# Strided and local attention with a layer-normed feed-forward: another order of the prologue and of chunk 0, and one piece of attention moved to chunk 1

## Chip, cores and metric

One core of a Trainium2 chip. The metric is the device time of one execution in microseconds (us); the median of three runs stands for a kernel. Engines: PE (matrix multiplication), DVE (vector), ACT (scalar functions), POOL (GpSimd) and SP, which here only issues DMAs; ACT issues some too. Every engine works its instructions in program order and waits on semaphores.

## The reference

```
scores = q @ k^T / sqrt(64)                      # q, k, v: (8, 8, 576, 64), float32
heads 0..3: keep 0 <= i - j < 32;  heads 4..7: keep j <= i with j % 32 == i % 32
attn = softmax(scores);  out = attn @ v          # heads side by side: x (8, 576, 512)
xn = (x - mean) / sqrt(var + 1e-6) * g_ln
y  = x + relu(xn @ w1) @ w2                      # w1 (512, 2048), w2 (2048, 512), float64
```

w1 and w2 come as float64; the kernel turns them into a high and a low part of float32 on the chip.

## The kernel before

**Pairs.** Attention goes by pairs of heads: 4 pairs in each of 8 batches, numbered 0 to 31, strided and local in turn (pair 0 strided, 1 local, 2 strided, 3 local). **Chunks.** The feed-forward goes by 9 chunks of 512 tokens: chunk c is the first 512 tokens of batch c, the last one what is left over of all batches. In a chunk it goes by 16 blocks f of 128 hidden units. A block is 12 matmuls into one PSUM bank `ph` (8 with the high part of w1, 4 with the low part), relu on ACT (`hh`), the rest on DVE (`hl`), and 12 matmuls into `po`.

**The list.** The prologue (batch 0) and chunk 0 (with batch 1's attention and all of the weights' preparation) follow a string `ORDER` of words `op:k:i:buffer`. Each word emits one step, and since every engine keeps program order, the list is each engine's order. The words:

- `T` turn the rows of q (i=0) or k (i=1) of pair k on PE, `c` copy them out of PSUM; `r` load raw q and k of a later pair, `tp` transpose them on DVE; `v` load v, `vs` copy v shifted by a block on POOL;
- `S` scores on PE, `mask`, `max` on DVE, `sub` (minus the maximum) on POOL, `exp` on ACT, `PP` transpose the probabilities on PE, `pt` copy them, `V` probabilities times v on PE, `den`, `xo` divide on DVE, `X` transpose the output on PE, `xh`, `xl` its high and low part, `st` store it;
- `W` load block k of both weights, and for weight i: `sc` scale the upper word on ACT, `low`/`lowA` shift the lower word on DVE or ACT, `mg` and `sg` put number and sign together on DVE, `hi` the high part on ACT, `lo` the low part on POOL; for w1 also `byg` (times g) and `add` (block sum) on POOL, `cm` column mean on PE, `cen` subtract it on DVE;
- `F` the 8 high matmuls of block k (`Fb` the last two of block 0, which need pair 3), `H` the 4 low ones, `hh`, `hl`, `G` the 12 matmuls of the block's second half; `xr`, `xs` the residual and its scale.

PSUM gives the prologue three rooms of two banks (buffers 0, 1, 2); a step that takes a room waits until the last reader of that room is done. There is one bank for `ph`.

**Before the list** stand the loads of batch 0: rows of q on SP and of k on ACT for pairs 1 to 3, pair 0's halves on both, then `gcol` and all of v on SP.

**Pieces.** From chunk 1 on a generator `pieces()` works batch 2 and later ones: in every block f one visit, after the block's first half (`ffn1`, `hh`, `hl`) and ahead of the second half of the block before. A piece i spans four visits: in the first S of pair i+1 and V of pair i on PE, mask to exp for pair i+1, the store of pair i and the load of v for pair i+2; in the second `x_raw` (pair i back from DRAM), the sums and the turn of pair i+1's probabilities through DRAM (`p_turned`), the transposition of q and k of pair i+3 and the load for pair i+4; in the third the load of the turned probabilities (`p_load`) and `x_blocks`; the fourth is empty. The first piece is i = 8; pair 8's scores and the turn of its probabilities (on PE, `PP:8`) stand in the list of chunk 0.

Of the kernel before, what the change touches and what calls it, by code (L numbers as in the profile page):

```python
# [26 lines left out]
hi:0:0 lowA:2:0 mg:1:0 hi:0:1 lo:0:0 F:0 exp:4 den:3 sg:1:0 lowA:3:0 lo:0:1 xo:3 sc:1:1 low:1:1
byg:1 X:3::1 mg:1:1 v:4 sg:1:1 add:1 PP:4::2 xh:3 sc:2:0 xl:3 cm:1::0 mg:2:0 Fb:0 pt:4 lowA:3:1
W:4 cen:1 H:0 lowA:2:1 sg:2:0 hi:1:0 tp:5 byg:2 V:4::0 hh:0 sc:2:1 add:2 hl:0 S:5::1 hi:1:1 st:1
mg:2:1 lo:1:0 cm:2::2 sg:2:1 F:1 W:5 mask:5 sc:3:0 lo:1:1 hi:2:1 cen:2 H:1 mg:3:0 hi:2:0 G:0  # L30
sg:3:0 hh:1 den:4 W:6 sc:3:1 hl:1 lowA:4:1 mg:3:1 lo:2:0 byg:3 lowA:4:0 F:2 sg:3:1 add:3 xo:4
sc:4:0 hi:3:1 W:7 mg:4:0 H:2 lo:2:1 lowA:5:0 sg:4:0 cm:3::0 G:1 cen:3 byg:4 sc:4:1 hi:3:0 mg:4:1
add:4 hh:2 sg:4:1 st:4 hl:2 sc:5:0 X:4::0 lo:3:0 F:3 mg:5:0 xh:4 r:6 lo:3:1 lowA:5:1 xl:4 H:3
sg:5:0 cm:4::0 hh:3 G:2 cen:4 byg:5 sc:5:1 hl:3 lowA:6:1 v:5 add:5 mg:5:1 hi:4:0 sg:5:1 lowA:6:0
lo:4:0 F:4 max:5 sc:6:0 lowA:7:0 mg:6:0 sub:5 lowA:7:1 cm:5::0 sg:6:0 H:4 cen:5 W:8 sc:6:1 byg:6
G:3 hh:4 mg:6:1 add:6 hi:4:1 hl:4 hi:5:0 sg:6:1 lo:5:0 cm:6::0 sc:7:0 F:5 cen:6 W:9 exp:5 lo:4:1
mg:7:0 hi:5:1 sg:7:0 H:5 tp:6 byg:7 sc:7:1 PP:5::0 lowA:8:0 G:4 add:7 st:0 hh:5 hi:6:0 hl:5 lo:5:1
pt:5 r:7 mg:7:1 hi:6:1 S:6::0 lo:6:0 sg:7:1 lowA:9:0 lowA:8:1 F:6 mask:6 sc:8:0 max:6 cm:7::0
mg:8:0 sg:8:0 sub:6 H:6 st:3 G:5 hh:6 cen:7 byg:8 st:2 hl:6 hi:7:0 lo:6:1 tp:7 sc:8:1 hi:7:1
V:5::0 add:8 lowA:9:1 r:8 F:7 mg:8:1 sg:8:1 lo:7:0 den:5 sc:9:0 xo:5 H:7 mg:9:0 sg:9:0 cm:8::0  # L40
hh:7 G:6 exp:6 byg:9 hl:7 W:10 sc:9:1 cen:8 add:9 mg:9:1 hi:8:0 PP:6::0 hi:8:1 sg:9:1 lo:8:0 F:8
tp:8 pt:6 W:11 lo:7:1 hi:9:1 cm:9::0 H:8 lo:8:1 sc:10:0 cen:9 lowA:10:0 G:7 lowA:10:1 mg:10:0 W:12
hi:9:0 sg:10:0 hh:8 byg:10 sc:10:1 hl:8 S:8::0 lowA:11:0 lo:9:0 mg:10:1 F:9 lowA:11:1 sg:10:1 v:6
add:10 mask:8 sc:11:0 H:9 mg:11:0 lo:9:1 lowA:12:1 sg:11:0 cm:10::0 G:8 hh:9 cen:10 byg:11 W:13
sc:11:1 hi:10:0 mg:11:1 hi:10:1 lo:10:0 hl:9 lowA:12:0 S:7::0 sg:11:1 add:11 sc:12:0 F:10 mask:7
W:14 lo:10:1 mg:12:0 cm:11::0 sg:12:0 H:10 max:7 sc:12:1 byg:12 G:9 hh:10 cen:11 st:5 add:12
mg:12:1 hi:11:0 hl:10 lowA:13:1 W:15 lo:11:0 sg:12:1 hi:11:1 cm:12::0 F:11 max:8 sc:13:0 lowA:13:0
cen:12 H:11 mg:13:0 hi:12:0 v:7 sg:13:0 lo:12:0 X:5::0 hh:11 G:10 xh:5 lo:11:1 sc:13:1 xl:5
lowA:14:1 hl:11 sub:7 hi:12:1 mg:13:1 V:6::0 lowA:14:0 r:9 byg:13 F:12 sg:13:1 den:6 add:13 xo:6
sc:14:0 H:12 lo:12:1 lowA:15:0 mg:14:0 exp:7 cm:13::0 sg:14:0 G:11 hi:13:1 cen:13 byg:14 xr:0  # L50
hh:12 sc:14:1 hl:12 lo:13:1 hi:13:0 mg:14:1 X:6::0 lo:13:0 sg:14:1 F:13 xh:6 add:14 xr:1 sc:15:0
xl:6 H:13 sub:8 mg:15:0 cm:14::0 hh:13 G:12 cen:14 xr:2 sg:15:0 hi:14:0 hl:13 byg:15 xs:0 PP:7::0
lo:14:0 F:14 pt:7 tp:9 st:6 lowA:15:1 add:15 sc:15:1 H:14 r:10 cm:15::0 hh:14 G:13 cen:15 exp:8
hl:14 hi:14:1 mg:15:1 hi:15:0 sg:15:1 lo:15:0 V:7::0 hi:15:1 xr:3 F:15 lo:15:1 den:7 xo:7 lo:14:1
xs:2 X:7::0 v:8 H:15 G:14 hh:15 xh:7 hl:15 xl:7 v:9 tp:10 PP:8::0 pt:8 xs:3 st:7 r:11 xs:1
# [972 lines left out]
```

## Time and profile before

| | us |
|---|---|
| median of 3 runs | 911.18 (909.15 to 911.70) |
| span of the profiled execution | 907.3 |
| median less span | 3.9 |
| PE busy | 884.9 |
| DVE, ACT, POOL busy | 435.4, 199.7, 147.9 |

The page comes from one profiled execution. PE's busy time counts overlapping matmuls once. The timeline lists instructions of one engine in order of time, and in square brackets how long the engine was idle before one and what ended that; "issue" means that it waited for nothing that the profile shows.

### The profile page before, as it was taken

The page shows a single profiled execution, that of the slowest core. Times are in us where ns is not written, and L with a number is a line of the kernel's source. Part 1 is how long each engine was busy: PE and PEld are TensorE (multiplying, and loading weights), DVE is VectorE, ACT ScalarE, POOL GpSimd, SP SyncE. Part 2 cuts the span into 40 slices and gives each one's busy share as a digit, 9 for nine tenths or more (in the row PEclk, how much of TensorE's full clock was granted, in tenths as well). Part 3 has the DMA queues.
Part 4 walks back from the last instruction along what each step waited for, and adds up shares of the span by engine and source line. Part 5 has one row for each costly group of instructions (what it writes and reads, how often), then busy time and mean ns, then how long its engine had stood idle before and what let it go on. Part 6 is the DMA issues. An engine that isn't in the chain of part 4 may idle for free.

```text
span 907.3 us, 18531 instructions
## 1 busy us (share of the span) xinstructions
PE 884.9 (98%) x7606; PEld 728.8 (80%) x7606; DVE 435.4 (48%) x864; ACT 199.7 (22%) x326; POOL 147.9 (16%) x186
## 2 busy tenths in 40 slices
PE   7699999999999999999999999999999999999997
PEld 6578787888888888888888888888888888888885
DVE  2888877544654455445644464445533321132113
ACT  3477663111111111111111111111111111111110
POOL 5477774000100011000100010001000000000000
PEclk8999999999999999999999999999999999999999
DMA  8887886675867575766666665757443230002001
GB/s 166 226 257 179 247 196 114 147 111 119 134 142 109 102 137 120 124 91 141 109 134 93 135 104 141 100 127 124 116 85 91 49 128 0 1 1 93 0 1 47
DMA packets 339621, 102.98 MB, mean 114 GB/s; under 512 B 276944, under 2 KB 331344, under 8 KB 339536
## 3 DMA queue, kind: packets, MB, share of 16 engines
q1 hardware_dynamic: 249920, 85.53, 42.9%
q10 hardware_dynamic: 89616, 16.26, 11.5%
q8 instruction: 60, 0.98, 0.5%
q14 instruction: 25, 0.20, 0.1%
...
## 4 chain that ended last, share of the span: by engine, by line
PE 93%; DMA 2%; DVE 1%; issue 1%; SPq 1%; POOL 1%; ACT 0%; DVEq 0%; POOLq 0%; ACTq 0%
PE po L775 42%; PE ph L748 28%; PE ph L755 14%; PE m L515 2%; PE m L445 2%; DMA s<-in_moe_w_ch_dram 1%; PE t L371 1%; PE s L445 1%; DMA rows<-in_q_dram 1%; PE av L515 1%; SPq L351 1%; PE cm L281 1%; PE px L636 0%; PE pp L501 0%; POOL r L270 0%
## 5 line engine op out<-in xcount | busy, mean ns | idle before, releaser
L775 PE MATMUL po<-w,hh 128*128 128x512 f32 x1152 | 359.2, 393 | 0.0
L765 DVE SCALAR_TENSOR_TENSOR hl<-ph,hh 128x512 fp32r<-128x512 f32 x144 | 99.3, 690 | 367.0 <-ACT hh L760 367.0
L775 PEld LDWEIGHTS po<-w,hh 128*128 128x128 f32 x1152 | 213.4, 188 | 44.8
L748 PE MATMUL ph<-xh,w 128*128 128x512 f32 x576 | 226.0, 392 | 1.4 <-ACT w L294 1.2
L775 PE MATMUL po<-w,hl 128*128 128x512 f32 x576 | 224.5, 390 | 0.0
L748 PE MATMUL ph<-xl,w 128*128 128x512 f32 x576 | 224.5, 390 | 0.0
L760 ACT ACTIVATE hh<-ph 128x512 fp32r<-128x512 f32 x144 | 86.1, 598 | 483.7 <-PE ph L755 469.0
L755 PE MATMUL ph<-xh,w 128*128 128x512 f32 x576 | 155.3, 392 | 0.0
L748 PEld LDWEIGHTS ph<-xh,w 128*128 128x128 f32 x576 | 108.3, 188 | 24.1 <-ACT w L294 1.4
L775 PEld LDWEIGHTS po<-w,hl 128*128 128x128 f32 x576 | 108.1, 188 | 23.1
L755 PEld LDWEIGHTS ph<-xh,w 128*128 128x128 f32 x576 | 108.2, 189 | 22.5 <-POOL w L298 0.2
L748 PEld LDWEIGHTS ph<-xl,w 128*128 128x128 f32 x576 | 108.3, 188 | 22.0
L491 POOL TENSOR_TENSOR sm<-sm,mx 128x648 f32<-128x648 f32 (+1 forms) x32 | 40.6, 1269 | 440.4 <-DVE mx L486 440.4
L723 POOL TENSOR_TENSOR rs<-rs,mhalf 128x1 f32<-128x1 f32 x36 | 19.7, 548 | 286.5 <-DVE rs L722 286.5
L497 ACT ACTIVATE sm<-sm 128x648 f32<-128x648 f32 (+1 forms) x32 | 23.8, 742 | 104.3 <-POOL sm L491 104.3
L298 POOL TENSOR_TENSOR w<-r,w 128x512 fp32r<-128x512 f32 x32 | 41.1, 1297 | 7.3 <-ACT w L294 6.9
L687 DVE TENSOR_TENSOR xl<-xo,xh 128x512 fp32r<-128x512 f32 x24 | 16.6, 692 | 38.8 <-ACT xh L686 38.8
L686 ACT ACTIVATE xh<-xo 128x512 fp32r<-128x512 f32 x24 | 15.2, 632 | 62.0 <-DMA pd<-sm 18.2
L486 DVE TENSOR_REDUCE mx<-sm 128x12 f32<-128x648 f32 (+1 forms) x32 | 26.3, 822 | 2.1
L565 DVE TENSOR_TENSOR xo<-m,den 64x64 f32<-64x64 f32 (+3 forms) x120 | 27.1, 289 | 0.0
L781 DVE SCALAR_TENSOR_TENSOR x<-po,rs,x 128x512 f32<-128x512 f32 x36 | 24.5, 737 | 2.0 <-PE po L775 1.8
L718 DVE BATCH_NORM_STATS2 st<-x 128x6 f32<-128x512 f32 x36 | 24.3, 674 | 0.0
...
## 6 DMA issues: line engine op xcount, KB each, us to landing
...
```

Source lines behind the costliest of these rows:

```text
L298: nc.gpsimd.tensor_tensor(out=t[:, 1], in0=self.w[i], in1=t[:, 0].bitcast(F32), op=ALU.subtract)
L445: nc.tensor.matmul(o, lhsT, rhs, start=True, stop=True, tile_position=(64 * h, pos))
L486: nc.vector.reduce_max(mx[:, :, 0:nt], sm, axis=AX.X)
L491: nc.gpsimd.tensor_tensor(out=sm, in0=sm, in1=mx[:, :, 0:nt].unsqueeze(3).broadcast_to([P, 2, nt, sm.shape[3]]), op=ALU.subtract)
L515: nc.tensor.matmul(at(h, t)[m * j:m * (j + 1)], self.p_cols(rows, t, j), self.v[rows, n, 0:w], start=True, stop=True, tile_position=(64 * ...
L565: nc.vector.tensor_tensor(out=xo[r, t0:t1, h0:h1].rearrange("p t h d -> p h t d"), in0=av, in1=den[r, h0:h1, t0:t1].unsqueeze(3).broadcast_to(
L748: nc.tensor.matmul(ph, w1h[:, cc], x[:, cc, :], start=(new and n == 0 and i == 0), stop=False)
L755: nc.tensor.matmul(ph, w1l[:, cc], xt[c][0][:, cc, :], start=False, stop=(cc == NCC - 1))
L760: nc.scalar.activation(out=hh, in_=ph, func=AF.Relu)
L765: nc.vector.scalar_tensor_tensor(out=hl, in0=ph, scalar=0.0, in1=hh.bitcast(F32), op0=ALU.max, op1=ALU.subtract)
L775: nc.tensor.matmul(po[i], hx[:, cs], w, start=(f == 0 and n == 0), stop=(f == NFC - 1 and n == 2))
L781: nc.vector.scalar_tensor_tensor(out=x, in0=po[i], scalar=rs, in1=x, op0=ALU.mult, op1=ALU.add)
```

## The change

All of `ORDER` is a new list. With it:

- the loads of batch 0 are words of the list now: `R` loads rows (pair 0's in halves on SP and ACT as before, k first; all others on SP), `g` loads `gcol`, `v` loads v; block 0 of the weights is loaded right behind the rows of pair 1;
- some steps go to DVE by a `D` behind the word: `cD` (two copies of turned rows), `addD` (block sum of block 0), `loD` (two low parts);
- pair 8's `S` to `pt` leave the list; piece 7, which has no pair of its own, does its scores in chunk 1's first visit, and its probabilities go through DRAM like those of later pairs. The pieces up to 11 have three visits, so chunk 1 holds five; the transposition and the load in the second visit are for pairs i+2 and i+3.

```diff
-T:0:0:0 T:0:1:1 c:0:0: c:0:1: T:1:0:2 S:0::0 c:1:0: T:1:1:2 mask:0 max:0 T:2:1:0 c:1:1: sub:0
+R:0:1 R:0:0 T:0:1:1 cD:0:1: R:1:1 T:0:0:0 c:0:0: T:1:1:2 R:1:0 S:0::0 mask:0 c:1:1: W:0 low:0:0
+max:0 T:1:0:1 R:2:1 sc:0:0 c:1:0: S:1::0 R:2:0 v:0 lowA:0:1 mg:0:0 sub:0 exp:0 sg:0:0 sc:0:1 T:2:1:2
...
     def m_piece(p, nxt):
-        ps = bank(f"m{p.id}")
+        ps = bank(f"m{(p or nxt).id}")
         parts = nxt.s_blocks(ps) if nxt else None
-        if p.k == 2 * NHP:
-            p.v_sums()
-        av = p.v_blocks(ps)
+        av = p.v_blocks(ps) if p else None
...
-    for p in first:
-        if p.k in BY_DVE:
-            p.load_qk(early.tile([P, 2 * S], F32, name=f"raw{p.id}"))
-        elif p.k == 0:
-            for i in range(2):
-                p.load_rows(i, nc.sync, slice(0, 1))
-                p.load_rows(i, nc.scalar, slice(1, 2))
-        else:
-            p.load_rows(0, nc.sync)
-            p.load_rows(1, nc.scalar)
-    nc.sync.dma_start(gcol, g_ln.rearrange("(c p) -> p c", p=P))
-    for p in first:
-        p.load_v(once=True)
...
     def one(op, k, i, buf):
         p = pairs[k]
-        if op == "T":
+        eng, copy = nc.gpsimd, nc.scalar.copy
+        if op.endswith("D"):
+            op, eng, copy = op[0:-1], nc.vector, nc.vector.tensor_copy
+        if op == "R":
+            if k == 0:
+                p.load_rows(i, nc.sync, slice(0, 1))
+                p.load_rows(i, nc.scalar, slice(1, 2))
+            else:
+                p.load_rows(i, nc.sync)
...
     def pieces():
-        for i in range(2 * NHP, NP):
+        for i in range(2 * NHP - 1, NP):
+            now = pairs[i] if i >= 2 * NHP else None
...
-            if i + 3 < NP:
-                pairs[i + 3].t_piece()
-            if i + 4 < NP:
-                pairs[i + 4].load_qk()
+            if i + 2 < NP:
+                pairs[i + 2].t_piece()
+            if i + 3 < NP:
+                pairs[i + 3].load_qk()
             yield
...
-            yield
+            if i >= 3 * NHP:
+                yield
```

Three places show what stands in a row now. **SP's queue at the start**; `rows_2`, `rows_0`, `rows_3`, `rows_1` are the rows of pairs 0, 1, 2, 3 (the names count heads), `s_` the weights, `raw_2` q and k of pair 4. Before:

```order
L361 DMA rows_2_235<-in_q_dram 96x3x128
L361 DMA rows_2_235<-in_k_dram 96x3x128
L361 DMA rows_0_240<-in_q_dram 96x6x128
L361 DMA rows_3_243<-in_q_dram 96x6x128
L361 DMA rows_1_246<-in_q_dram 96x6x128
L813 DMA gcol<-in_moe_g_ln_dram 128x4x1
```

After:

```order
L360 DMA rows_2_235<-in_k_dram 96x3x128
L360 DMA rows_2_235<-in_q_dram 96x3x128
L360 DMA rows_0_254<-in_k_dram 96x6x128
L360 DMA rows_0_254<-in_q_dram 96x6x128
L222 DMA s_0_311<-in_moe_w_ch_dram 128x4x256
L225 DMA s_0_312<-in_moe_w_ch_dram 128x1024
L360 DMA rows_3_331<-in_k_dram 96x6x128
L360 DMA rows_3_331<-in_q_dram 96x6x128
```

Pair 1's k rows moved from ACT to SP, block 0 of the weights came up to stand behind pair 1, and v stands behind pair 2's rows.

**ACT's queue around the first relu** (`hh_0`); `w_1` is block 1's high part (the first of the two is w1's), `s_` and `p_` the weights' words in preparation. Before:

```order
L251 ACTIVATE s_3_765<-s_3_765 128x512
L251 ACTIVATE s_2_709<-s_2_709 128x512
L294 ACTIVATE w_1_905<-r_1_848 128x512
L760 ACTIVATE hh_0_935<-ph_0_838 128x512
L244 ACTIVATE p_2_937<-s_2_709 128x512
```

After:

```order
L292 ACTIVATE w_2_914<-r_2_910 128x512
L242 ACTIVATE p_3_916<-s_3_781 128x512
L249 ACTIVATE s_3_781<-s_3_781 128x512
L755 ACTIVATE hh_0_933<-ph_0_897 128x512
L292 ACTIVATE w_1_935<-r_1_720 128x512
```

The first steps on block 3 (`p_3`, `s_3`) stand right ahead of `hh_0` and of block 1's high part now.

**DVE's queue from `hl_1` to `hl_2`**, which frees the bank for the next block. Before:

```order
L765 SCALAR_TENSOR_TENSOR hl_1_1048<-ph_1_994,hh_1_1038 128x512
L258 SCALAR_TENSOR_TENSOR p_3_1046<-p_3_1046,s_3_765 128x512
L264 SCALAR_TENSOR_TENSOR r_3_1064<-s_3_765,p_3_1046 128x512
L565 TENSOR_TENSOR xo<-av_910,den_213 128x2x6x64
L258 SCALAR_TENSOR_TENSOR p_4_1069<-p_4_1069,s_4_893 128x512
L264 SCALAR_TENSOR_TENSOR r_4_1084<-s_4_893,p_4_1069 128x512
L284 TENSOR_TENSOR r_3_1036<-r_3_1036,cm_1086 128x512
L258 SCALAR_TENSOR_TENSOR p_4_1102<-p_4_1102,s_4_894 128x512
L264 SCALAR_TENSOR_TENSOR r_4_1111<-s_4_894,p_4_1102 128x512
L765 SCALAR_TENSOR_TENSOR hl_2_1115<-ph_2_1055,hh_2_1109 128x512
```

After:

```order
L760 SCALAR_TENSOR_TENSOR hl_1_1057<-ph_1_1012,hh_1_1052 128x512
L256 SCALAR_TENSOR_TENSOR p_4_1054<-p_4_1054,s_4_870 128x512
L262 SCALAR_TENSOR_TENSOR r_4_1076<-s_4_870,p_4_1054 128x512
L483 TENSOR_REDUCE mx_0_1082<-sm_208 128x2x5
L256 SCALAR_TENSOR_TENSOR p_4_1109<-p_4_1109,s_4_871 128x512
L262 SCALAR_TENSOR_TENSOR r_4_1122<-s_4_871,p_4_1109 128x512
L663 TENSOR_TENSOR xl_1119<-px_1084,xh_1118 128x30x16
L663 TENSOR_TENSOR xl_1119<-px_1084,xh_1118 128x2x16
L256 SCALAR_TENSOR_TENSOR p_5_1131<-p_5_1131,s_5_886 128x512
L262 SCALAR_TENSOR_TENSOR r_5_1155<-s_5_886,p_5_1131 128x512
L760 SCALAR_TENSOR_TENSOR hl_2_1160<-ph_2_1091,hh_2_1139 128x512
```

Preparation runs about one block further ahead of the relus, and pair 4's low part `xl` stands between them earlier.

## Rows read from the trace of the kernel before

**Rows 1.** The page: busy time of each engine, its share of the span, instructions.

```profile
PE 884.9 (98%) x7606; PEld 728.8 (80%) x7606; DVE 435.4 (48%) x864; ACT 199.7 (22%) x326; POOL 147.9 (16%) x186
```

**Rows 2.** PE's timeline, 0 to 60 us: start, duration, instructions, [idle before <-releaser].

```profile
8.28 1.21 PE L371 MATMUL t<-ident,rows 96*64 96x96 f32 x24 [1.68 <-DMA rows<-in_q_dram]
...
16.28 0.88 PE L445 MATMUL s<-kt_l,qt_l 64*32 64x64 f32 x38 [3.09 <-issue]
...
28.65 0.76 PE L515 MATMUL av<-v_l,pt 64*32 64x65 f32 x52 [1.27 <-issue]
29.21 0.99 PE L445 MATMUL s<-kt_l,qt_l 64*32 64x64 f32 x75
33.03 0.31 PE L445 MATMUL s<-kt_l,qt_l 64*32 64x64 f32 x5 [2.83 <-issue]
...
37.89 0.77 PE L501 MATMUL pp<-ident,sm 128*128 128x128 f32 x5 [1.78 <-ACT sm L497]
...
44.27 0.50 PE L748 MATMUL ph<-xh,w 128*128 128x512 f32 x1 [1.19 <-ACT w L294]
...
54.70 0.47 PE L748 MATMUL ph<-xh,w 128*128 128x512 f32 x1
```

**Rows 3.** Busy us by stage: PE, PEld, DVE, ACT, POOL (instructions), PE's clock, DMA, GB/s.

```profile
5.30:54.70 49.40, 34.47 (x929) 28.87 (x925) 30.20 (x52) 26.08 (x40) 24.04 (x33) 0.86 0.87 208
54.70:92.20 37.50, 37.50 (x295) 30.68 (x294) 32.56 (x51) 26.44 (x46) 30.34 (x33) 1.00 0.79 211
92.20:155.20 63.00, 62.72 (x536) 50.53 (x527) 48.31 (x83) 35.50 (x61) 42.32 (x44) 1.00 0.79 191
```

**Rows 4.** Groups by line and shape, 5 to 60 us: busy us, mean ns.

```profile
L258 DVE SCALAR_TENSOR_TENSOR p<-p,s 128x512 uint32<-128x512 uint32 x8 | 5.5, 687 | 0.2
...
L667 DVE TENSOR_TENSOR xl<-px,xh 128x512 fp32r<-128x512 f32 x2 | 1.4, 680 | 0.0
...
L251 ACT ACTIVATE s<-s 128x512 uint32<-128x512 uint8 x6 | 3.8, 669 | 0.0
...
L383 ACT COPY qt_s<-t 128x576 f32<-128x576 f32 x2 | 2.5, 1240 | 5.0 <-PE t L371 5.0
...
L407 POOL COPY v_l<-v_l 32x1088 f32<-32x1088 f32 x4 | 4.4, 1109 | 0.2
L491 POOL TENSOR_TENSOR sm<-sm,mx 128x648 f32<-128x648 f32 x3 | 3.8, 1273 | 8.6 <-DVE mx L486 8.6
```

**Rows 5.** Timelines of ACT and SP, 0 to 60 us: the issue of loads (start, duration).

```profile
1.21 2.95 ACTq L361 DMA_DIRECT2D rows<-in_k_dram  x4
4.20 1.28 ACT L383 ACT_TABLE_LOAD   x1 [4.20 <-DMA rows<-in_q_dram]
```

**Rows 6.** Moved GB/s in 40 slices of 0 to 42 us.

```profile
GB/s 0 42 250 272 213 231 227 208 231 214 230 161 120 86 50 219 152 130 73 151 207 241 378 350 181 128 28 137 128 140 345 392 327 418 388 383 388 229 42 128
```

**Rows 7.** DMA queues from 30.0 to 33.1 us: PE's instruction queue (packets, MB).

```profile
q8 instruction: 1, 0.02, 2.7%
```

**Rows 8.** Timelines of PE and ACT in chunk 1: S, V, and the loads of `pt`.

```profile
178.99 0.91 PE L445 MATMUL m<-kt_s,qt_s 64*64 64x54 f32 x44
179.83 0.97 PE L515 MATMUL m<-v_l,pt 64*32 64x64 f32 x72
...
202.72 0.97 PE L445 MATMUL m<-kt_l,qt_l 64*32 64x64 f32 x72
...
192.09 2.42 ACTq L628 DMA_DIRECT2D pt<-pd  x4
...
218.06 0.38 ACTq L623 DMA_DIRECT2D pt<-pd  x1
```

More of the change, by code (lines that the diff above doesn't have):

```diff
@@ L27 @@
[L27 to L55, printed above, removed]
-"""
-BY_DVE = ()
@@ L59 @@
-ONCE = False
+R:0:1 R:0:0 T:0:1:1 cD:0:1: R:1:1 T:0:0:0 c:0:0: T:1:1:2 R:1:0 S:0::0 mask:0 c:1:1: W:0 low:0:0
+max:0 T:1:0:1 R:2:1 sc:0:0 c:1:0: S:1::0 R:2:0 v:0 lowA:0:1 mg:0:0 sub:0 exp:0 sg:0:0 sc:0:1 T:2:1:2
+mask:1 mg:0:1 sg:0:1 R:3:0 max:1 PP:0::0 c:2:1: T:2:0:1 cD:2:0: pt:0 sub:1 V:0::0 T:3:0:2 g:0 den:0
+byg:0 hi:0:1 c:3:0: xo:0 R:3:1 addD:0 S:2::1 X:0::2 cm:0::0 mask:2 T:3:1:1 exp:1 xh:0 max:2 cen:0
+PP:1::0 lo:0:1 c:3:1: sub:2 S:3::1 r:4 hi:0:0 pt:1 exp:2 xl:0 v:1 tp:4 PP:2::0 lo:0:0 pt:2 W:1
@@ new lines @@
+S:4::2 mask:3 lowA:1:0 vs:1 sc:1:0 max:3 mask:4 v:3 mg:1:0 V:1::0 v:2 W:2 den:1 sg:1:0 xo:1 sub:3
+lowA:1:1 exp:3 sc:1:1 mg:1:1 r:5 PP:3::2 max:4 X:1::0 sg:1:1 V:2::1 pt:3 W:3 vs:3 xh:1 den:2 hi:1:1
+xo:2 lowA:2:0 sc:2:0 v:4 V:3::2 X:2::1 xl:1 den:3 byg:1 mg:2:0 sub:4 exp:4 xh:2 lo:1:1 xo:3 PP:4::0
+W:4 lowA:2:1 W:6 sg:2:0 X:3::2 W:5 sc:2:1 xl:2 add:1 mg:2:1 F:0 xh:3 xl:3 pt:4 cm:1::2 sg:2:1 Fb:0
+hi:2:1 sc:3:0 H:0 W:7 tp:5 cen:1 lowA:3:0 byg:2 add:2 hh:0 hi:1:0 mg:3:0 S:5::0 cm:2::2 V:4::1 hl:0
@@ new lines @@
+sg:3:0 lo:2:1 lo:1:0 F:1 cen:2 lowA:3:1 sc:3:1 lowA:4:0 den:4 st:3 mask:5 H:1 xo:4 byg:3 hi:2:0
+add:3 lowA:4:1 cm:3::0 W:8 mg:3:1 sg:3:1 hh:1 sc:4:0 cen:3 hl:1 G:0 hi:3:1 mg:4:0 sg:4:0 lo:2:0
+hi:3:0 lowA:6:0 max:5 X:4::0 F:2 r:6 sc:4:1 st:0 st:1 lo:3:1 mg:4:1 byg:4 xh:4 sg:4:1 lowA:5:0 xl:4
+sub:5 add:4 lo:3:0 sc:5:0 lowA:6:1 mg:5:0 H:2 hh:2 G:1 cm:4::0 sg:5:0 byg:5 hi:4:1 hl:2 sc:6:0 F:3
+mg:6:0 st:2 low:7:1 lowA:5:1 sg:6:0 add:5 v:5 H:3 cen:4 exp:5 cm:5::0 G:2 lowA:7:0 sc:7:0 hi:4:0 W:9
+hh:3 mg:7:0 sg:7:0 sc:5:1 cen:5 low:8:0 hl:3 byg:6 mg:5:1 lowA:8:1 sg:5:1 lo:4:1 add:6 byg:7 lo:4:0
@@ new lines @@
+cm:6::0 F:4 hi:5:0 H:4 sc:7:1 cen:6 lo:5:0 hi:5:1 mg:7:1 PP:5::0 sg:7:1 hi:6:0 tp:6 G:3 sc:8:0
+mg:8:0 hh:4 sg:8:0 pt:5 hl:4 sc:6:1 add:7 st:4 hi:7:1 W:10 lo:6:0 S:6::0 F:5 mg:6:1 mask:6 lo:5:1
+byg:8 sg:6:1 max:6 cm:7::0 cen:7 lo:7:1 H:5 sc:8:1 W:11 G:4 sub:6 mg:8:1 hi:6:1 hi:7:0 sg:8:1
+low:9:0 hh:5 sc:9:0 add:8 V:5::0 hl:5 mg:9:0 hi:8:1 sg:9:0 den:5 lowA:9:1 exp:6 lo:7:0 lo:8:1 sc:9:1
+lowA:10:0 xo:5 byg:9 mg:9:1 r:7 sg:9:1 F:6 cm:8::0 cen:8 sc:10:0 H:6 hh:6 W:12 add:9 hi:9:1 mg:10:0
+sg:10:0 lowA:10:1 lo:6:1 G:5 sc:10:1 lowA:11:0 hi:8:0 hl:6 PP:6::0 mg:10:1 lo:9:1 pt:6 F:7 byg:10
@@ new lines @@
+lo:8:0 H:7 sg:10:1 sc:11:0 low:11:1 cm:9::0 G:6 hi:10:1 mg:11:0 sg:11:0 lo:10:1 cen:9 add:10 hh:7
+sc:11:1 mg:11:1 byg:11 hi:9:0 lowA:12:0 lo:9:0 W:13 hl:7 cm:10::0 sg:11:1 tp:7 add:11 F:8 cen:10
+st:5 H:8 sc:12:0 S:7::0 hi:11:1 mg:12:0 low:12:1 sg:12:0 G:7 mask:7 hi:10:0 sc:12:1 mg:12:1 hh:8
+lowA:13:0 hl:8 sg:12:1 W:14 lowA:13:1 sc:13:0 lo:11:1 cm:11::0 cen:11 byg:12 F:9 mg:13:0 H:9 lo:10:0
+sg:13:0 W:15 add:12 hi:12:1 max:7 lowA:14:0 sc:13:1 cm:12::0 hi:11:0 mg:13:1 lowA:14:1 byg:13 cen:12
+sg:13:1 G:8 hh:9 hl:9 X:5::0 sc:14:0 sub:7 hi:12:0 hi:13:1 lo:11:0 F:10 H:10 add:13 loD:12:1 mg:14:0
@@ L368, in t_rows @@
             for a in range(NA):
-                for c in range(2):
+                for c in range(CC):
                     for h in range(2):
@@ L906, in one @@
         elif op == "lo":
-            split(k).rest(i)
+            split(k).rest(i, eng)
         elif op == "F":
@@ L939, in pieces @@
             yield
-            pairs[i].x_raw(nc.scalar)
+            if now:
+                now.x_raw(nc.scalar)
             if nxt:
@@ L950, in pieces @@
                 nxt.p_load()
-            pairs[i].x_blocks()
+            if now:
+                now.x_blocks()
             yield
-            yield
+            if i >= 3 * NHP:
+                yield
     gen = pieces()
```

74 lines of the change are left out of this document (39 added, 35 removed).

## Prediction, made without the result

> **What bounds the kernel now.** I read the page first, then the matmul engine's (PE's) timeline, then the busy time by stage, then the queues. The page gives a span of 907.3 us, and PE is busy 98% of it [rows 1]. PE's timeline shows that all of its waits over 0.3 us lie ahead of 54.70, where the second feed-forward block of chunk 0 (F:1) starts without a wait [rows 2]; from 54.7 to 92.2, the start of F:7, PE is busy 37.50 of 37.50 us, and from there to the first visit of chunk 1 at 155.2 62.72 of 63.00 [rows 3]. From 5.3 to 54.7 it is busy only 34.47 of 49.40 us [rows 3]. So the end moves by four things alone: when F:1 starts, new waits after it, PE work that is added or dropped, and new waits in chunk 1. The time outside the span is 911.18 - 907.3 = 3.9 us against the median of the three runs, and I add it unchanged.
>
> **Term 1: the start of F:1.** PE has the same work ahead of F:1 in both lists, so what changes is waiting. I follow the longest chain through the new list, with the durations of [rows 4].
>
> The first load: before, S:0 stands behind T:1:0, which waits for its q rows until 8.28 and takes 1.21 [rows 2], so S:0 can't start before 9.4. After, T:1:1 stands there, whose load is the first behind pair 0's. ACT issues two loads instead of five (five took until 4.16), so its table load of 1.28 ends near 3.0 and not 5.5 [rows 5]. T:0:1 is copied on DVE (a price that no row shows: between 0.68, DVE reading as many PSUM columns densely, and 1.24, ACT's price for this strided copy; I take 0.95, and nobody waits for it). The q copy on ACT ends near 7.9, S:0 starts at 8.0, mask and max end at 11.3 with the shift of W:0 between them, the subtraction on POOL (1.27) at 12.8, the exponential at 13.6.
>
> S:1 needs T:1:0 and ends near 14.5, with a wait of 3 us in it as before; before it ended at 17.2 [rows 2]. From there the matrices go round three PSUM rooms. With 0.15 us for each hand-over, PP:0 starts at 15.8, V:0 at 18.0, S:3 ends at 27.0 (before 33.3), and PP:3 starts at 31.6 (37.89) [rows 2]. The gain comes mostly from T:2 and T:3, each cut into halves between other work, and from the shifted copies of v on POOL (2 x 1.11 each [rows 4]), which now stand behind the subtractions that gate the chain.
>
> Then DVE carries the chain, almost without a gap: den, xo, the second max, the halves of x, until xl:2 at 42.4 and xl:3 at 43.7. F:0 starts at 41.2 (44.27 [rows 2]), H:0 ends at 45.1, cen:1 on DVE ends at 46.4, hi:1:0 on ACT at 47.0, V:4 on PE at 47.8, and F:1 starts at 48.0 instead of 54.70: 6.7 us.
>
> Does the data come in time? ACT's queue is the place that decides: sc:3:0 and lowA:3:0 now stand ahead of hh:0 and hi:1:0, so F:1 waits for W:3 to land. Up to W:3 SP moves 2.36 MB of rows, 1.18 of v, 1.18 of raw q and k (pair 5's load of 0.59 moved ahead of W:3) and 4.19 of weights: 8.9 MB. Before, the core moved 208 GB/s on average from 5.3 to 54.7 [rows 3], and 220 to 270 for the first rows, 350 to 420 for weights [rows 6]. At 208 that is 42.8 us after the first issue at about 0.7, and with some 1.5 for the first and last latency W:3 lands at about 45. Four ACT steps of about 0.67 [rows 4] follow: F:1 at 48. The two chains arrive together, with no slack between them. A walk leaves out all small gaps, so I take **1.0** off: **-5.7** us.
>
> Three of PE's waits before are put down to "issue": 3.09, 1.27 and 2.83 us [rows 2]. One 16 KB packet of PE's instruction queue lies in the stretch of the last one [rows 7], and between the second and the third stand 52 + 75 matmuls, each with its weight load: 254 instructions. The new list has the same small matmuls, so I keep such waits in it, of 1.3 to 3 us each, in S:1, S:3, V:1 and V:3; of the last three some 3 us in all lie on the chain, the rest beside work of DVE and POOL. The Trainium skill ("Runtime: NRT & Kernel Launch", Instruction fetch mechanics) says that the sequencer fetches the next 16 KiB block of 256 instructions while it executes the current one and that crossing a boundary is mostly hidden; the trace disagrees for runs of such short matmuls, with 7.2 us of waits, and by that rule the sum would be some 3 us lower.
>
> **Term 2: from F:1 to F:7.** There is one PSUM bank for ph, so F:k+1 waits until DVE has read ph for hl:k. Before, DVE is busy 32.56 of 37.50 us in this stretch with 51 instructions [rows 3]. The new list puts more preparation ahead of F:7: four magnitudes, three signs and one centring more (8 x 0.69 = 5.5 [rows 4]), one more den and xo (1.2), three shifts on DVE (1.5), one pair of local transposes less (-1.5). That makes 39.3 us of DVE for 37.5 + 0.9 = 38.4 us of PE (one more V block). So DVE becomes the bound here by about 0.9, and its own idle time (4.9 us before; most of it vanishes when it is the bound) adds something. I take **+1.5**; bounds 0 and +4. After F:7 DVE has 5 us less to do than before, and was busy only 48.31 of 63.00 us [rows 3], so nothing more is lost there.
>
> ACT and POOL carry about the same as before; what moves to DVE (one block sum, two rests) relieves POOL at places where PE isn't waiting.
>
> **Term 3: PE work.** The six transposes of PP:8 go (0.6 to 0.7), the copy pt:8 on ACT too; S:8 only moves from chunk 0 into the first visit of chunk 1. In exchange pair 8's probabilities take the way through DRAM that all later pairs take. **-0.65**.
>
> **Term 4: chunk 1 in visits of three.** Before, S of one piece starts at 178.99 and of the next at 202.72 [rows 8], four visits apart; without the 1.8 us of S and V that is 5.48 a visit, so with three the next V comes 18.3 us after this one. A strided pair's pt load is issued on ACT from 192.09 to 194.5, a local one's at 218.06 [rows 8]; with three visits V would want them at 179.83 + 18.3 = 198.1 and 203.6 + 18.3 = 221.9, so 3.6 and 3.5 us after the last issue. The landing itself isn't in the trace. A local load is 320 KB on a shared queue: 1.5 us at 220 GB/s, 3 at half of it, plus latency. So it is near the edge: 0 to 1 us for each of four pieces. I take **+0.8**, bounds 0 and +4. Pair 8's own load stands behind chunk 0's four stores on SP, but v's loads are ahead of them and there is no store of pair 7's output any more. From chunk 2 on all is one visit earlier, which gives slack.
>
> **Sum:** -5.7 + 1.5 - 0.65 + 0.8 = -4.05: a span of 903.2, and **907.1 us** as measured.
>
> **Rivals.**
> (a) DVE as bound keeps its old rhythm. If it is busy only 87% (32.56 of 37.50) also when it has 39.3 us to do, F:1 to F:7 takes 45.2 us instead of 38.4: +6.8 in place of +1.5, less what DVE gains by running ahead when PE is late (some 2.5). 910 us. Against it: DVE idles now mostly because it waits for PE.
> (b) Chunk 1's three visits are too short: 3.6 us do not cover the pt load, each of four pieces loses 1 us: +4 in place of 0.8: 910.3.
> (c) The one queue is late, and this one ends slower. All rows now go through SP but for pair 0's, and 1.05 MB of weights stand ahead of T:2's. If the 8.9 MB come at 170 GB/s instead of 208, W:3 lands at 54.5, F:1 starts at 57.2, term 1 is +2.5, term 2 vanishes, and with terms 3 and 4 the time is 913.8. It decides against the change below about 180 GB/s. For it: v's loads ran at 50 to 160 GB/s for most of 11.5 to 20 us [rows 6]. Against it: their packets are small and SP was busy issuing them, while weights on the same single queue reached 350 to 420.
> (d) PE's instruction blocks are there in time in the new order: no waits in S:3, V:1, V:3, 3 us less: 904. The mechanism needs PE to be slower than the fetch, and only three of the seven blocks fetched up to 60 us show a wait before. This is what the rule of the Trainium skill cited in term 1 would give.
> (e) The change doesn't do what it says. Read in the code, it does: piece 7 with no pair of its own, then 3 visits each up to piece 11, 15 of chunk 1's 16 visits. No chance of its own.
>
> **How the numbers follow.** The forecast 0.52 (own range 904 to 909), (a) 0.18, (b) 0.10, (c) 0.13, (d) 0.07. A measurement tells about 0.3% from no change, 2.7 us: faster is below 908.45, slower above 913.9. Of the forecast 0.45 lies below that bound; (d) lies below it whole, (a) and (b) by 0.03; that is 0.55 faster. Of (c) most lies above 913.9, with its worse cases: 0.11 slower. The rest, 0.34, is the same. For eight in ten the range runs from the forecast with (d)'s gain and no loss in terms 2 and 4, 902, to the near side of (c), 912.5.
>
> **What would show it.** Right: F:1 at 47 to 50, hh:0 not waiting for W:3 longer than 1 us, DVE busy over 90% between F:1 and F:7, PE waits for hl of 1 to 2 us in total there, V in chunk 1 with waits of under 1 us each. Wrong: F:1 after 52 (then see whether ACT's sc:3:0 waits for DMA, or PE for "issue"), PE idle between F:1 and F:7 of over 4 us, or a wait of PE for pt in chunk 1 of over 2 us.

## Result and the profile after

The changed kernel takes 922.15 us (median of 4 runs, 921.26 to 924.36), the kernel before 910.16 in the same comparison: ratio 1.0149 [1.0120, 1.0177], so 13.5 us slower by the ratio (the two medians alone differ by 12.0). The forecast was 907.1, in a range of 902.0 to 912.5. The profiled span went from 907.3 to 921.0 us. Page of after, busy time of the engines, beside [rows 1]:

```profile
PE 888.6 (96%) x7600; PEld 730.6 (79%) x7600; DVE 440.9 (48%) x874; ACT 196.5 (21%) x321; POOL 145.2 (16%) x182
```

PE's busy time grew by 3.7 us with less work to do, so 10 of the 13.7 us of span are idle time and the rest is matmuls that take longer. After: PE's waits by what ended them (us in total, times, longest), the first five of the list:

```profile
PE po L770 <- DVE x L776: 7.0, 5, 1.4
PE s L442 <- issue: 4.7, 1, 4.7
PE pp L498 <- DVE r L282: 3.8, 2, 3.5
PE av L511 <- issue: 3.0, 2, 1.6
PE m L511 <- DMA pt<-pd: 2.9, 4, 0.9
```

The first, third and fifth are new. Where they stand in the span is seen best from one marker, the start of the relu `hh` on ACT (us). At chunk 2, block 1 both kernels have done the same pairs, apart from the six transposes of `PP:8`:

| `hh` of | before | after | after less before |
|---|---|---|---|
| chunk 0, block 1 | 57.73 | 56.24 | -1.5 |
| chunk 0, block 10 | 115.91 | 113.76 | -2.2 |
| chunk 0, block 12 | 128.64 | 132.16 | +3.5 |
| chunk 2, block 1 | 257.96 | 263.33 | +5.4 |
| chunk 3, block 1 | 353.09 | 360.24 | +7.2 |
| chunk 7, block 1 | 730.68 | 744.28 | +13.6 |

**The prologue.** After, PE's timeline in S:1, and from V:4 to F:1 (start, duration, [idle before <-releaser]):

```profile
11.31 0.87 PE L442 MATMUL s<-kt_l,qt_l 64*32 64x64 f32 x66 [0.74 <-ACT qt_l L379]
16.91 0.46 PE L442 MATMUL s<-kt_l,qt_l 64*32 64x64 f32 x14 [4.72 <-issue]
...
51.83 0.92 PE L511 MATMUL av<-v_s,pt 54*64 54x65 f32 x46 [0.64 <-DMA v_s<-in_v_dram]
52.68 0.50 PE L743 MATMUL ph<-xh,w 128*128 128x512 f32 x1
```

F:1 starts at 52.68, not at 48.0 (54.70 before [rows 2]). S:1 comes to its stop earlier than before (12.2 against 13.2) and leaves it later (16.91 against 16.28 [rows 2]). In either kernel the stop is behind PE's 222nd matmul, and the DMA records show what comes just ahead of its end: one 16 KB packet of PE's own instruction queue, from 13.69 to 15.11 us here and from 13.48 to 14.69 before. After, that queue from 13.6 to 15.2 us (packets, MB, share of 16 engines):

```profile
q8 instruction: 1, 0.02, 5.5%
```

From F:1 to F:7 (after, busy us of PE, PEld, DVE, ACT, POOL, PE's clock, DMA, GB/s):

```profile
52.68:91.18 38.50, 38.50 (x307) 31.60 (x302) 36.65 (x59) 29.11 (x51) 34.36 (x37) 1.00 1.00 276
```

DVE is at 95% there, and PE doesn't wait at all.

**The end of chunk 0.** After, PE and then DVE around `PP:7`:

```profile
129.09 1.33 PE L498 MATMUL pp<-ident,sm 128*128 128x128 f32 x5 [3.45 <-DVE r L282]
130.07 2.05 PE L750 MATMUL ph<-xh,w 128*128 128x512 f32 x4
```

```profile
127.34 0.69 DVE L713 BATCH_NORM_STATS2 st<-x 128x6 f32<-128x512 f32 x1 [4.09 <-DMA x<-xds]
...
128.36 0.68 DVE L282 TENSOR_TENSOR r<-r,cm 128x512 f32<-128x512 f32 x1
```

DVE stands idle for 4.09 us until the residual of `xs:1` has landed; behind it in program order is `cen:14` (L282), which empties the PSUM room that `PP:7` needs. The residual's loads were issued at 120.0 to 122.2. Behind the wait PE is slow as well: the granted clock is 0.83 from 126 to 136, a mean of its two levels, 1.2 and 2.4 GHz; it is at the lower one from 128.7 to 132.2.

**The start of every later chunk.** After, PE and DVE at the start of chunk 2:

```profile
262.17 1.07 PE L750 MATMUL ph<-xh,w 128*128 128x512 f32 x4
264.63 0.70 PE L770 MATMUL po<-w,hh 128*128 128x512 f32 x2 [1.40 <-DVE x L776]
```

```profile
260.31 0.79 DVE L606 STREAM_TRANSPOSE sm<-sm 128x640 f32<-128x640 f32 x1
261.02 1.22 DVE L417 STREAM_TRANSPOSE qt_s<-raw 128x576 f32<-128x576 f32 x1
262.08 1.24 DVE L417 STREAM_TRANSPOSE kt_s<-raw 128x576 f32<-128x576 f32 x1
263.16 2.64 DVE L776 SCALAR_TENSOR_TENSOR x<-po,rs,x 128x512 f32<-128x512 f32 x4
```

Before, PE (S and V of the visit in block 0, then chunk 2's first `po`) and DVE at the same place:

```profile
250.25 0.97 PE L445 MATMUL m<-kt_l,qt_l 64*32 64x64 f32 x72
251.15 1.04 PE L515 MATMUL m<-v_s,pt 54*64 54x64 f32 x44
...
257.70 0.62 PE L775 MATMUL po<-w,hh 128*128 128x512 f32 x2
```

```profile
255.19 2.71 DVE L781 SCALAR_TENSOR_TENSOR x<-po,rs,x 128x512 f32<-128x512 f32 x4
```

`finish` (L776, before L781) reads the old chunk's `po` and so frees it for the new one. It now stands behind the sums and transpositions of a piece's second visit, and starts 2.6 us after PE is done with the old `po` (before, 0.1). The same wait of 1.40 us is there at 361.54, 458.29, 555.06 and 651.86. Before, block 0 of a chunk had the first visit, whose S and V keep PE busy for 2 us while DVE goes on to `finish`: no wait. Chunk 1 now holds five pieces of three visits, 15 in 16 blocks, so piece 12 starts in chunk 1's last block and all later chunks begin with a second visit.

**Chunk 1.** After, two of PE's four waits for `pt`, and the issue of the load on ACT for the second:

```profile
175.48 0.81 PE L511 MATMUL m<-v_s,pt 54*64 54x64 f32 x40 [0.90 <-DMA pt<-pd]
...
212.77 0.81 PE L511 MATMUL m<-v_s,pt 54*64 54x64 f32 x40 [0.41 <-DMA pt<-pd]
```

```profile
205.87 2.21 ACTq L624 DMA_DIRECT2D pt<-pd  x4
```

### The profile page after: what moved, and what is told of

It reads as the page before. It is cut to its first block, busy times and chain, and to the rows that moved or that the text cites. A ratio compares the mean times of both kernels' runs of the same rounds, so it can differ in the third digit from the quotient of the medians.

```text
span 921.0 us, 18511 instructions
## 1 busy us (share of the span) xinstructions
PE 888.6 (96%) x7600; PEld 730.6 (79%) x7600; DVE 440.9 (48%) x874; ACT 196.5 (21%) x321; POOL 145.2 (16%) x182
## 4 chain that ended last, share of the span: by engine, by line
PE 79%; DMA 9%; DVE 5%; SPq 4%; issue 1%; ACTq 0%; POOL 0%; ACT 0%; DVEq 0%; POOLq 0%
PE po L770 37%; PE ph L743 24%; PE ph L750 12%; PE m L511 2%; DMA pt<-pd 2%; SPq L350 2%; PE m L442 2%; DMA v_s<-in_v_dram 2%; DMA s<-in_moe_w_ch_dram 2%; DMA xds<-xo 1%; DVE x L776 1%; SPq L398 1%; DMA pd<-sm 1%; DVE kt_s L417 1%; DVE qt_s L417 1%
## 5 line engine op out<-in xcount | busy, mean ns | idle before, releaser
L296 POOL TENSOR_TENSOR w<-r,w 128x512 fp32r<-128x512 f32 x30 | 39.1, 1313 | 3.4 <-ACT w L292 3.4
L681 ACT ACTIVATE xh<-xo 128x512 fp32r<-128x512 f32 x24 | 15.2, 632 | 54.0 <-DVE xo L598 34.0
L776 DVE SCALAR_TENSOR_TENSOR x<-po,rs,x 128x512 f32<-128x512 f32 x36 | 24.2, 731 | 2.1 <-PE po L770 1.8
```

Of the source, the lines that this page charges most:

```text
L296: eng.tensor_tensor(out=t[:, 1], in0=self.w[i], in1=t[:, 0].bitcast(F32), op=ALU.subtract)
L776: nc.vector.scalar_tensor_tensor(out=x, in0=po[i], scalar=rs, in1=x, op0=ALU.mult, op1=ALU.add)
```

## Experiments

Each is the changed kernel with the edit shown, if nothing else is said. "Gain" is the difference of its ratio from 1.0149, times 907 us. Each interval reaches some 0.2%, about 2 us, to either side, so a gain of a few us is judged by the trace as well.

| kernel | median us | ratio to before | gain, us |
|---|---|---|---|
| changed kernel | 922.15 | 1.0149 [1.0120, 1.0177] | |
| finish first | 918.74 | 1.0127 [1.0106, 1.0148] | 2.0 |
| realigned | 914.12 | 1.0073 [1.0052, 1.0094] | 6.9 |
| pieces alone | 919.99 | 1.0144 [1.0120, 1.0167] | 0.5 |
| scale later | 916.50 | 1.0100 [1.0077, 1.0122] | 4.4 |
| load after pt | 924.36 | 1.0179 [1.0158, 1.0200] | -2.7 |
| three edits | 910.88 | 1.0035 [1.0017, 1.0053] | 10.3 |
| list alone | 911.08 | 1.0037 [1.0024, 1.0051] | 10.2 |
| v:4 early | 921.09 | 1.0147 [1.0128, 1.0166] | 0.2 |
| list, both words moved | 906.09 | 0.9984 [0.9969, 0.9998] | 15.0 |
| list, scale moved | 907.58 | 0.9995 [0.9977, 1.0013] | 14.0 |
| k rows on ACT | 932.08 | 1.0262 [1.0236, 1.0289] | -10.2 |

### Which half of the change costs: the pieces alone, the list alone

The pieces alone: the kernel before with its own list, pair 8's words and those that the new pieces do themselves taken out, and the new `m_piece` and `pieces`.

```diff
-... S:8::0 ... mask:8 ... max:8 ... sub:8 ... exp:8 ... v:9 tp:10 PP:8::0 pt:8 ... r:11
-        for i in range(2 * NHP, NP):
+        for i in range(2 * NHP - 1, NP):
```

> The kernel before with its own list, only pair 8's words (S to pt, V's load and transposition that the new pieces do themselves) taken out and the new pieces of chunk 1 (five, of three visits) put in; the prologue's order is the old one. Theory (the pieces cost, the new list's prologue gains a little): boundaries +8.4, waits for the turned probabilities +2.9, matmuls of PP:8 -0.65, so about 10.5 above the kernel before, 920.7. Rival (the new prologue and chunk 0 cost most of it): within 4 us of the kernel before.

Measured: 1.0144 [1.0120, 1.0167], 13.1 us above before and 2.6 more than expected; the list doesn't enter it. The five waits for `po` of 1.40 us are there, and 3.2 us for `pt`. The longest of these, of PE in the last block of chunk 1, costs twice, since the matmuls behind it are slow (granted clock 0.50 from 250.4 to 253.9):

```profile
249.80 0.86 PE L515 MATMUL m<-v_s,pt 54*64 54x64 f32 x40 [1.69 <-DMA pt<-pd]
250.59 1.22 PE L774 MATMUL po<-w,hh 128*128 128x512 f32 x2
```

The list alone: the new list with the old pieces, pair 8's words put back.

```diff
-cen:15 hi:15:0 F:13 H:13 V:7::0
+cen:15 S:8::0 hi:15:0 mask:8 F:13 max:8 sub:8 H:13 V:7::0
...
-hl:15
+hl:15 v:9 tp:10 PP:8::0 pt:8 r:11
```

> The other half of the change alone: the new list with the old pieces (four visits each, the first with S and V of pairs 9 and 8), so that pair 8's words are put back into the list (S:8 behind cen:15, PP:8 at the end, and the loads and transpositions of pairs 9 and 10). Theory (the pieces cost all but 1 us of it, since they alone cost 12.5): 0 to 2 us above the kernel before, with the wait ahead of PP:7 in it. Rival 1 (the list gains what F:1 gains, 2 us or more): 2 to 4 us below the kernel before. Rival 2 (pair 8's steps collide with the scale and the residual at the end of chunk 0): 3 to 6 above.

Measured: 1.0037 [1.0024, 1.0051], 3.4 us above before, in the second rival's range. At chunk 2, block 1 the marker stands at 260.69, 2.7 above before, and that stays to the end (733.63 against 730.68). The wait ahead of `PP:7` is in it with 3.17 us, and S:8 waits 0.8 for `cen:15`, which the rival had named in kind. The two halves add up to 16.5 us, the change to 13.5. The difference of 3.0 us is no more than the three intervals allow (some 2.6, 2.1 and 1.2 us either way), so it needs no cause of its own.

### The chunk's start: finish first, and realigned

```diff
+            late = f == 0 and c > 1 and c + 1 < B
             if c + 1 < B:
-                next(gen, None)
+                if not late:
+                    next(gen, None)
...
             second(*prev)
+            if late:
+                next(gen, None)
```

> The changed kernel; only at the start of chunks 2 to 6 (f = 0) the visit is put behind the second half of the last block and its finish, so that DVE does finish (which frees po) ahead of the visit's sums and transpositions. Theory (po is held by DVE's work of the second visit, which now falls on f = 0): the five waits of PE for po of 1.40 us each vanish, and with the low clock behind them, 1.68 us a boundary, the time falls by 5 x 1.68 = 8.4 us from 922.2 to about 913.8. Rival (the boundary is longer for another reason, for example more work of PE in it, or the wait only turns up one visit later): 921 to 923, with waits of PE on the visit's steps in place of those on po.

Measured: 2.0 us less by the ratios, whose intervals overlap, so the trace has to decide. That is a quarter of the theory's 8.4. No wait for `po` is left, but five others have come, of 0.77 us each. The low clock that the theory put behind the waits isn't there in the changed kernel either: its granted clock is 1.00 from 132.2 to 917.2. First PE at the start of chunk 2, then DVE:

```profile
265.20 0.50 PE L743 MATMUL ph<-xh,w 128*128 128x512 f32 x1 [0.77 <-DVE hl L760]
```

```profile
257.75 2.76 DVE L776 SCALAR_TENSOR_TENSOR x<-po,rs,x 128x512 f32<-128x512 f32 x4
...
263.38 1.25 DVE L417 STREAM_TRANSPOSE kt_s<-raw 128x576 f32<-128x576 f32 x1
264.46 0.69 DVE L760 SCALAR_TENSOR_TENSOR hl<-ph,hh 128x512 fp32r<-128x512 f32 x1
```

Now the visit's work stands ahead of the next `hl`, which frees `ph`. From chunk 2 to chunk 7 the marker loses 5.4 us against before instead of 8.2. So the order behind `po` is only half of it: DVE has the second visit and `finish` in two blocks in which PE has nothing but the feed-forward.

```diff
-            if i >= 3 * NHP:
+            if i >= 3 * NHP - 1:
                 yield
```

> The changed kernel; only piece 11 has its fourth, empty visit back, so that chunk 1 holds 16 visits and piece 12 starts with chunk 2, as before. Theory (the phase of the pieces against the chunks is what costs): the five waits for po vanish as before the change, 913.8, with the waits for the turned probabilities in chunk 1 as they are except piece 11's. Rival (phase is not the cause): 921 to 923.

Measured: 6.9 us less; from chunk 2 to chunk 7 0.6 us are lost instead of 8.2. No wait for `po` or `ph` is left. The theory holds: the phase of the pieces against the chunks was the cause. PE and then DVE at the start of chunk 2:

```profile
259.64 1.07 PE L750 MATMUL ph<-xh,w 128*128 128x512 f32 x4
260.55 0.62 PE L770 MATMUL po<-w,hh 128*128 128x512 f32 x2
```

```profile
258.04 2.71 DVE L776 SCALAR_TENSOR_TENSOR x<-po,rs,x 128x512 f32<-128x512 f32 x4
```

ACT still waits in places for the store of the turned probabilities ahead of a load of `pt` (5.42 us in chunk 3). The kernel before has such waits too (12.0 us in four, from chunk 2 on), and PE stands idle for none of them. The 0.6 us that are left I have not traced.

### The end of chunk 0: the scale later

```diff
-... hi:15:1 xs:1 F:12 cen:14 hi:14:0 PP:7::0 pt:7 H:12 add:15 hh:12
-xs:0 G:11 cm:15::0 tp:8 hl:12 lo:15:1
+... hi:15:1 F:12 cen:14 hi:14:0 PP:7::0 pt:7 H:12 add:15 hh:12
+G:11 cm:15::0 tp:8 hl:12 xs:1 xs:0 lo:15:1
```

> The changed kernel with two words of the list moved: xs:1 and xs:0 (scale and sums of the residual on DVE) stand behind hl:12 and no longer ahead of cen:14. Theory (DVE, in program order, waits for the residual's load ahead of cen:14, and PP:7 on PE needs cen:14's room): the wait of 3.45 us ahead of PP:7 and the low clock behind it vanish, 3.5 to 4.5 us, 918. Rival (PP:7 is held by something else in the chain, or the wait comes back at the next step that needs DVE): less than 1 us.

Measured: 4.4 us less. PE comes to `PP:7` without a wait and stays fast:

```profile
125.61 0.71 PE L498 MATMUL pp<-ident,sm 128*128 128x128 f32 x5
126.07 1.17 PE L750 MATMUL ph<-xh,w 128*128 128x512 f32 x4
127.08 0.62 PE L770 MATMUL po<-w,hh 128*128 128x512 f32 x2
```

From `PP:7` to the next `po` it takes 127.08 - 125.61 = 1.47 us here and 131.92 - 129.09 = 2.83 in the changed kernel: the wait of 3.45 costs 1.4 more in slow matmuls.

### Chunk 1: the load after pt

```diff
-            if i + 3 < NP:
+            if i + 3 < NP and i >= 3 * NHP:
                 pairs[i + 3].load_qk()
             yield
             if nxt:
                 nxt.p_load()
+            if i < 3 * NHP:
+                pairs[i + 3].load_qk()
```

> The changed kernel; only in chunk 1 the load of q and k of pair i+3 (8 issues on SP) is made in the third visit, behind the load of the turned probabilities, and no longer in the second visit ahead of it. Theory (the turned probabilities share the queues and the 16 engines with those 8 loads, which makes them late): the four waits of PE for pt in chunk 1, 2.9 us in all, fall to 0 to 1, and the time by 2 to 3.5 us against the changed kernel. Rival (the time is that of the chain sums, store, load itself, which three visits don't cover): waits and time unchanged within 0.5 us. A second rival: the later load makes the next transposition late, waits of PE for the scores instead, slower by 1 to 3.

Measured: 2.7 us more; neither the theory's gain nor a wait for the scores. The waits put down to `pt` fall from 2.9 to 1.1 us, but one of 3.75 us has come ahead of V of a local pair. PE, then SP and ACT:

```profile
233.42 0.96 PE L511 MATMUL m<-v_l,pt 64*32 64x64 f32 x72 [3.75 <-DMA raw<-in_k_dram]
```

```profile
226.93 3.08 SPq L350 DMA_DIRECT2D raw<-in_q_dram  x4
230.05 3.56 SPq L350 DMA_DIRECT2D raw<-in_k_dram  x4
```

```profile
227.56 0.35 ACTq L619 DMA_DIRECT2D pt<-pd  x1
```

V doesn't read `raw`; of what it reads, `pt` was issued last. Written behind it in the program, the load was issued 0.6 us ahead of it in time, because SP doesn't wait for ACT; the two then move together, and V goes on 5.9 us after the issue of `pt`. This speaks for a transfer that is slowed by its neighbours, and the packets of ACT's queue bear it out: the last one of this load ends 4.7 us after its issue, with SP's queue moving 107 GB/s beside it. The same load takes 3.15 us in the changed kernel (67 GB/s beside it), and a local pair's in chunk 2 of the kernel before 2.5 (22 GB/s). Whether three visits can ever be enough stays open.

### Three edits together

Realigned, scale later and load after pt in one kernel.

> The changed kernel with three edits together: piece 11 with its fourth visit back, the residual's scale behind hl:12, the load of q and k behind that of the turned probabilities in chunk 1. The single edits gave 6.9 and 4.5 us for the first two; the third is expected to give 2 to 3.5. Theory (three separate losses that add up): 13 to 15 us below the changed kernel, which is the kernel before within 2 us. Rival (one loss hides behind another): 9 to 11 us below the changed kernel.

Measured: 10.3 us less, and still 0.35% above before. The number lies in the rival's range, but the theory fails by its third edit alone, which costs here too (a wait of 2.37 us for a local pair's `pt` at 223.79): the three measured by themselves add up to 6.9 + 4.4 - 2.7 = 8.6. So no loss hides behind another; they can be taken away one by one, and even then the kernel is not faster than before.

### The prologue: S:1's stop, and the loads ahead of F:1

```diff
-WAKE = 6
+WAKE = 0
```

> The changed kernel without the 12 wake matmuls at PE's start (24 instructions less ahead of everything with their weight loads; they only fill a scratch bank). In the profiles of the changed kernel and of the experiments so far PE stops inside S:1 behind its 66th matmul, for 0 to 4.7 us, with nothing that the profile shows as the cause. Theory (PE waits for its own next block of instructions, whose place is a count of instructions): the stop moves 12 matmuls on, to behind the 78th of S:1's 80, or out of S:1 into the next step. Rival (it is a wait for data or for a semaphore of S:1): it stays behind the 66th.

One run of 923.42 us. PE in S:1:

```profile
12.98 1.02 PE L442 MATMUL s<-kt_l,qt_l 64*32 64x64 f32 x78 [0.74 <-ACT qt_l L379]
16.65 0.30 PE L442 MATMUL s<-kt_l,qt_l 64*32 64x64 f32 x2 [2.65 <-issue]
```

The stop is behind the 78th matmul. That of V:1 moved from behind the 20th to behind the 32nd, that of V:3 from the 9th to the 21st. The place is a count of instructions, not a step: again the 222nd matmul. PE waits for its own next instructions, and goes on 1.6 us behind the end of the packet of its instruction queue (15.03). The Trainium skill ("Runtime: NRT & Kernel Launch", Instruction fetch mechanics) says that crossing into the next 16 KiB block is mostly hidden; these runs disagree for short matmuls, with 2.65 us here and 4.72 in the changed kernel.

```diff
-lowA:1:1 exp:3 sc:1:1 mg:1:1 r:5 PP:3::2 ... xo:2 lowA:2:0 sc:2:0 v:4 V:3::2
+lowA:1:1 exp:3 sc:1:1 mg:1:1 v:4 r:5 PP:3::2 ... xo:2 lowA:2:0 sc:2:0 V:3::2
```

> The changed kernel; only the load of v for pair 4 is moved ahead of the load of q and k of pair 5 and of block 3 of the weights on SP's queue. Theory (V:4, right ahead of F:1 on PE, waits for this load: 0.64 us in the profile of the changed kernel, 1.72 in that of the first experiment, where S:1 had no wait): the wait vanishes, F:1 starts 0.6 to 1.7 us earlier and the time falls by as much. Rival (block 1's high part, or block 3 of the weights, which land later by what is moved ahead of them, hold F:1 next): F:1 within 0.3 us, no change.

Measured: 0.2 us less, no difference that can be told; the rival. F:1 came 1.3 us earlier in this profile, but S:1 had left its stop 1.3 us earlier too (15.65), so the edit gave nothing. V:4 no longer waits, but block 3's weights land later. They hold ACT (`p` of block 3, ahead of `hh:0`), and so `hl:0` and F:1. PE, then ACT:

```profile
51.41 0.47 PE L743 MATMUL ph<-xh,w 128*128 128x512 f32 x1 [1.19 <-DVE hl L760]
```

```profile
48.70 0.64 ACT L242 ACTIVATE p<-s 128x512 f32<-128x512 f32 x1 [1.55 <-DMA s<-in_moe_w_ch_dram]
```

```diff
-                p.load_rows(i, nc.sync)
+                p.load_rows(i, nc.scalar if i else nc.sync)
```

> The changed kernel; only the k rows of pairs 1 to 3 are issued on ACT's queue, as before the change, and not on SP's. What holds F:1 beside PE's own stop is the load of v for pair 4, or block 3 of the weights where that load goes first. Theory A (the 16 DMA engines are full: busy 0.88 to 1.06 of the time from 2 to 52 us in the changed kernel): the bytes are the same, so F:1 moves by less than 0.5 us. Theory B (one queue's issue rate is the limit): loads behind the rows come earlier, F:1 by 1 to 2 us, the time too. Against both: three issues on ACT's queue of 0.4 us each ahead of the first copies, up to 1.2 us later.

Measured: 10.2 us more; both theories missed. On ACT an issue waits behind ACT's copies, which wait for PE, which waits for rows. PE has three waits for k rows, 15.6 us in all, the longest ahead of the last turn:

```profile
38.26 2.19 PE L370 MATMUL t<-ident,rows 96*64 96x96 f32 x24 [9.80 <-DMA rows<-in_k_dram]
```

So it doesn't tell whether the queue or the 16 engines limit the loads. It shows that in this list the rows belong on SP, which waits for nobody.

### The list, mended

The list alone with the scale moved as above, without and with `v:4` moved.

> As the kernel with both words moved, but the load of v for pair 4 stays where the new list has it. Theory: 906.6, the other one 0 to 1 lower. Rival (block 3 of the weights is made late by what is moved ahead of it): this one is the lower.

> The new list with the old pieces, as in the experiment on the list alone, and two words moved in it: the residual's scale behind hl:12 (4.5 us in the changed kernel) and the load of v for pair 4 ahead of that of q and k of pair 5. Theory (the loss ahead of PP:7 is the list's only one, its gain at F:1 stays): 911.1 - 4.5 = 906.6 and up to 1 less for the load, so 0.5 to 2 below the kernel before. Rival (pair 8's steps at the end of chunk 0 set it, not the scale): within 1 us of the experiment on the list alone.

Measured: 0.9995 [0.9977, 1.0013] and 0.9984 [0.9969, 0.9998]. Both are some 3.5 us or more below the list alone, as the theory says; the second is the only kernel here that is below the kernel before, by 1.5 us, with the interval just clear of 1; as one of twelve comparisons that is weak evidence. Between the two there is no difference that can be told. The profile of the first, which fell on a short execution (span 902.3), shows what the prologue does when PE doesn't stop in S:1:

```profile
14.51 1.41 PE L442 MATMUL s<-kt_l,qt_l 64*32 64x64 f32 x80 [0.74 <-ACT qt_l L379]
...
48.20 0.93 PE L511 MATMUL av<-v_s,pt 54*64 54x65 f32 x48
49.06 0.50 PE L744 MATMUL ph<-xh,w 128*128 128x512 f32 x1
```

F:1 starts at 49.06, with no wait for loads ahead of it.

## Why the prediction was wrong

The predicted span was 903.2 us, the measured one 921.0, so 17.8 more. By its own steps:

- **Term 1** (F:1 5.7 us earlier): it was 2.0 in this profile, so 3.7 are missing. The step that failed is "S:1 ends near 14.5, with a wait of 3 us in it as before". I took the stop for a duration. It is an arrival. In all 14 profiles a 16 KB packet of PE's instruction queue starts at 12.1 to 13.8 us and ends at 13.4 to 15.1, wherever PE stands by then; what sets its start isn't shown. Where PE came to the end of its 222nd matmul at 11.8 to 15.3, it went on at 14.7 (load after pt) to 16.9 (changed kernel), each time 1.3 to 1.8 us behind the packet's end; where it came at 15.7 or later (finish first; list, scale moved; k rows on ACT) it did not stop. An earlier S:1 only waits longer. From there the chain ran in the order that I walked, 3 to 5 us late.

  The second bound was the loads: I checked W:3 against ACT and left out `v:4`, which is behind it on SP. With either one first, the other can hold F:1 (v:4 early), in the mild form of rival (c): not slower than before, but the end of the gain.

  How much of the 3.7 is chance is open: in the eight profiles with the same list up to F:1, F:1 started at 48.95 (three edits) to 52.68 (changed kernel, the latest), so the gain was 2.0 to 5.8 us, and the forecast lies at the good end of that. In the best one PE still stopped in S:1 until 15.79, but its granted clock stayed at 1.00 from 22.3 on, while the changed kernel's is 0.50 from 40.0 to 46.8.
- **Term 2** (F:1 to F:7, +1.5 on 38.4): PE took 38.50 us and waited for nothing, so the loss was 0.1. "So DVE becomes the bound here by about 0.9" failed: DVE ran ahead, and in this stretch did 36.65 us of work, not 39.3 (three steps of preparation more than before, not eight). PE's extra work was not a V block, which stands in the stretch before as well, but the six transposes of `PP:6`. Rival (a) fell with it.
- **"After F:7 DVE has 5 us less to do than before ... so nothing more is lost there"** failed: 3.45 us of wait ahead of `PP:7` and 1.4 of slow matmuls, shown by the scale-later run. I judged DVE by its busy share. It was idle, but in program order behind a load that had not landed.
- **Term 3** (-0.65) was not measured by itself; PE has 6 matmuls less on the page.
- **Term 4** (+0.8, bounds 0 to +4): 2.9 us of waits, inside the bounds and nearer to rival (b). The mechanism was right, the size was off: "3.6 and 3.5 us after the last issue" is too short, since V went on 3.5 to 5.2 us after it.
- **"From chunk 2 on all is one visit earlier, which gives slack"** is the step that turned the sign. One visit earlier puts the second visit where the first had been, ahead of `finish`, and costs 1.6 us at each of five chunks, 8.2 in all (the marker from chunk 2 to chunk 7), shown by the realigned run, which takes nearly all of it back. I had the DVE times of the visits and of `finish` in reach and didn't lay them against the blocks.

These are 3.7 - 1.4 + 4.8 + 2.1 + 8.2 = 17.4 of the 17.8 in the profiled execution; the rest is not accounted for. It is not slow matmuls behind the waits for `pt`, as in the pieces-alone run: there the granted clock is 1.00 in this profile. The sign was lost in the parts of the program that I had called free. The bounds of term 4 were wide enough; for the chunk's start I had set none.
